# A fused attention and feed-forward kernel: strides, load rows, table loads and a new written order

## The chip, the cores and the metric

The kernel runs on one core of a Trainium2 chip, in one launch. The metric is the device time of an execution in microseconds (us); the number compared is the median over repeated executions. Before the change it is 213.36 us, the median of three (212.89, 213.36, 214.8). A separate execution was recorded by the hardware profiler, and all lines of profile in this text come from such records.

Names: TensorE (PE in the profile, PEld for its weight loads), VectorE (DVE), ScalarE (ACT), GpSimd (POOL), SyncE (SP). A name with a q (SPq, ACTq) is an engine's sequencer, which among other things issues DMAs.

## The reference

q, k and v are [8, 8, 576, 64] (batch, heads, positions, head size) in fp32. Each head's scores decay with distance; then a feed-forward layer runs over all 4608 tokens, with 512 columns in, 1024 inside and 512 out.

```python
scores = (1 / np.sqrt(64)) * np.matmul(q, k.transpose(0, 1, 3, 2))
gamma = 1.0 - 2.0 ** (-5.0 - np.arange(H))
Dmat = np.where(rel >= 0, gamma[:, None, None] ** rel[None, :, :], 0.0)   # rel = row - column
x = np.matmul(scores * Dmat, v)             # then [4608, 512], heads side by side
h = x @ w_in
e = np.exp(h - h.max(-1, keepdims=True))
solu = h * (e / (e.sum(-1, keepdims=True) + 1e-09))
ln = (solu - solu.mean(-1, keepdims=True)) / np.sqrt(var + 1e-06) * g_ln   # var: of solu over the row
out = ln @ w_out
```

## The kernel before

**Tiling.** The tokens are cut into 18 pairs n of 256 (two neighbouring positions on a partition): sixteen pairs of one batch entry each, and two tails (n = 8 and n = 17) that hold the last 64 positions of four entries. Each pair is worked through in two halves of 128 tokens (i = 0 or 1). The attention is done in chunks: products inside a chunk, plus a running state per head that is carried from chunk to chunk. The state gives the long-range part.

**Steps.** Each step is a short function, and a text called ORDER lists all of them, about a thousand words, in one sequence. A word is a step's name, its indices, and an engine letter where there is a choice: `q:0.1@v` is the cast of q of pair 0, half 1, on VectorE (v), ScalarE (s) or GpSimd (g). A loop at the end calls the steps in the order of the text. Each engine executes its own instructions strictly in that order; between engines semaphores are placed where data or buffers require it. So the order on each engine and on each DMA queue is written out by hand, and no scheduler changes it.

The steps that matter here:

- `lq`, `lk`, `lv` load 512 KB of q, k or v of a pair (L173, from SyncE's queue); `wi:a` loads 128 rows of w_in (L647), `wo:a` two blocks of rows of w_out (L667). The loads share 16 buffers.
- `q`, `k`, `v` cast to fp16 (L152 and L150 are the copy helper, L197 multiplies by a decay from the table `small`).
- `tp` transposes q and k of a pair on TensorE (L239), `qkT` copies the result to SBUF; `sc` are the scores (L265), `mk` the causal mask (L276, VectorE); `kp` the chunk's contribution to the state (L290); `t`, `s32`, `s16` the state itself, in fp32 and fp16; `xs` (L349) and `xv` (L364) the two products that make x; `xT` copies it to SBUF.
- `mm1` is x @ w_in (L426, L416), `max` its negated row maximum (L434), `exp` the exponential (L449), `solu` the product h * e (L497), `nmu` the negated mean (L507), `sq` the sum of squares (L517), `w1`, `w2`, `pow` the scale of a row.
- `lpj` transposes (L584), `uTj` copies, `mm2` is the second product (L607), `osb` scales its rows and `st` stores them (L634, L639). The last half is done in two halves of columns (`mm2:17.1.0`, `mm2:17.1.1` and so on).
- `cwA`, `cwB` cast one quarter of w_in in two halves (cast_w_in, through the copy helper); `ws` multiplies blocks of w_out by g_ln, `mean` and `mc` take their mean, `cw` subtracts it; `g32` scales g_ln.
- `warm:k` issues k products of zeros, 128x128 by 128x512, into a bank that nothing reads (L726). The zeros are the last slice of the tile s16s, which VectorE clears (L853).
- `gx` fills a table of decays with four exponentials on ScalarE (L734).

**Layout of w_in and w_out.** Before, the cast of w_in also permutes its 1024 columns: column 8p + c goes to place 128c + p, so the cast reads fp32 numbers 32 bytes apart. To match, row 8p + c of w_out is on partition p, in block c; a load of two blocks reads 4 KB in one piece per partition. g_ln is loaded as [128, 8] with 8 numbers in a row per partition.

**Start.** Ahead of the loop stand two loads from ScalarE's queue, `small` (L850) and g_ln (L851), then the constants: the clearing of s16s, `ones` and `mhalf` on VectorE, and `place`, `ident` (identity for the transposes) and `tris` (causal masks) on GpSimd. ORDER starts after that.

Of the kernel before, what the change touches and what calls it, by code (L numbers as in the profile page):

```python
# [12 lines left out]
P = 128  # L13
# [33 lines left out]
def kernel(  # L47
# [62 lines left out]
    T = {}  # L110
# [552 lines left out]
    @step  # L663
    def wo(a, i, j, eng):
        t = load_tile("wo").rearrange("p (c m) -> p c m", c=2)
        w = moe_w_out.rearrange("(p c) m -> p c m", p=P)
        nc.sync.dma_start(out=t, in_=w[:, 2 * a : 2 * a + 2])  # L667
        T["w_out32", 2 * a], T["w_out32", 2 * a + 1] = t[:, 0], t[:, 1]
# [50 lines left out]
    @step  # L719
    def warm(k, i, j, eng):  # L720


        junk = psum[:, int(BANKS[turns.get("bank", -1) + 1])]
        zeros = s16s[:, 2 + 6 - 1].rearrange("p a e d -> p (a e d)")
        for _ in range(k):
            nc.tensor.matmul(  # L726
                out=junk, lhsT=zeros[:, 0:P], rhs=zeros, start=True, stop=True
            )
# [3 lines left out]
    def gx_(n, i, j, eng):  # L732
# [12 lines left out]
        lk:0 gx lq:0 k:0.0@s k:0.1@g q:0.0@v lv:0 lq:1 q:0.1@v warm:21 tp:0 v:0.1@v v:0.0@v kp:0  # L745
        q:1.1@v t:0.0@v s32:0.0 qkT:0.1@v qkT:0.0@s lk:1 k:1.0@v q:1.0@g warm:6 sc:0.0 t:0.1 wi:2
        k:1.1@s sc:0.1 wi:0 wi:3 s32:0.1 mk:0.1.0 warm:4 tp:1 mk:0.0.0 mk:0.0.1 cwB:2@s s16:0.0@s
        mk:0.1.1 xv:0 cwA:2@g wi:1 qkT:1.1@v cwA:0@v cwB:0@g xT:0.0@v cwB:3@g qkT:1.0@s sc:1.0
        mk:1.0.1 xs:0.1 cwA:3@s mm1:0.0.3 lv:1 cwA:1@g xT:0.1@v s16:0.1@g cwB:1@s v:1.1@g mk:1.0.0
        sc:1.1 mm1:0.0.0 lq:2 lk:2 q:2.1@g q:2.0@g mk:1.1.0 mm1:0.1 v:1.0@v mk:1.1.1 k:2.0@g  # L750
        max:0.1 exp:0.1 mm1:0.0.2 mm1:0.0.1 max:0.0 k:2.1@v kp:1 t:1.0@s warm:7 tp:2 s32:1.0 lv:2
        solu:0.1 v:2.1@v exp:0.0 s16:1.0@g qkT:2.1@s qkT:2.0@s t:1.1 v:2.0@g nmu:0.1 solu:0.0
        xs:1.1 lq:4 xv:1 lv:3 lq:3 lk:3 xT:1.0@s nmu:0.0 warm:2 sc:2.1 sc:2.0 mk:2.1.0 xT:1.1@s
        kp:2 q:4.1@g q:4.0@g s32:1.1 mk:2.0.0 t:2.0@s mk:2.1.1 mk:2.0.1 uc:0.1@s sq:0.1 mm1:1.1
        s32:2.0 uc:0.0@v sq:0.0 max:1.1 xv:2 mm1:1.0 q:3.0@v xT:2.0@s exp:1.1 s16:2.0@g t:2.1
        xs:2.1 max:1.0 xT:2.1@s solu:1.1 mm1:2.0 lpj:0 q:3.1@g max:2.0 wo:2 wo:0 v:3.0@g g32
        k:3.1@g exp:1.0 mm1:2.1 solu:1.0 ws:4@s k:3.0@s wo:1 exp:2.0 w1:0@g v:3.1@g ws:0@g wo:3
        ws:1@g ws:5@g ws:2@s w2:0 uTj:0.1@v uTj:0.0@v ws:3@s max:2.1 lk:4 w1:1@v nmu:1.1 nmu:1.0
        ws:6@s warm:4 kp:3 ws:7@g t:3.0@s tp:3 solu:2.0 uc:1.0@v mm2:0.0 s32:3.0 qkT:3.0@s exp:2.1
        s32:2.1 qkT:3.1@s lv:4 pow:0 t:3.1 k:4.1@s sq:1.0 mean k:4.0@g sc:3.1 sc:3.0 solu:2.1  # L760
        nmu:2.0 mm2:0.1 v:4.1@v mc@s mk:3.1.0 mk:3.1.1 s16:3.0@g v:4.0@g lk:5 lk:6 mk:3.0.1
        mk:3.0.0 sq:1.1 uc:1.1@s tp:4 s32:3.1 kp:4 lq:5 qkT:4.0@s cw:5@g xv:3 qkT:4.1@s osb:0.1@v
        xs:3.1 t:4.0 warm:4 lpj:1 xT:3.1@s lq:6 cw:6@v sc:4.0 k:6.1@g nmu:2.1 xT:3.0@v s32:4.0
        k:5.1@g lv:5 uTj:1.1@s s16:1.1@s cw:0@v uTj:1.0@s osb:0.0@s t:4.1 mk:4.0.0 uc:2.0@v mm1:3.0
        w2:1 k:5.0@g q:5.1@g mm1:3.1 q:5.0@g pow:1 v:5.0@g s16:4.0@g max:3.0 uc:2.1@v s32:4.1 lk:7
        sc:4.1 q:6.0@s q:6.1@s mk:4.0.1 v:5.1@g mm2:1.0 exp:3.0 max:3.1 st:0.1 lv:6 mk:4.1.0
        mk:4.1.1 mm2:1.1 xv:4 w1:2@g xs:4.1 v:6.0@g solu:3.0 k:6.0@s v:6.1@g osb:1.0@s exp:3.1
        solu:3.1 dt:5 kp:5 t:5.0 osb:1.1@s xs:4.0 tp:6 st:1.0 s16:2.1@g cw:1@v st:0.0 sq:2.0 kp:6
        xT:4.1@s t:6.0 warm:2 lpj:2 s32:5.0 qkT:6.1@v t:5.1 xT:4.0@s qkT:6.0@s uTj:2.1@s cw:4@g
        sc:5.1 sc:5.0 uTj:2.0@s nmu:3.1 lq:8 mk:5.1.1 cw:7@v mk:5.1.0 sq:3.1 k:7.0@s sq:2.1 cw:3@v  # L770
        mk:5.0.0 mm1:4.0 max:4.0 lv:8 cw:2@g w2:2 pow:2 s32:6.0 mm1:4.1 s16:5.0@g exp:4.0 s16:6.0@g
        lq:7 mm2:2.1 lv:7 max:4.1 mk:5.0.1 solu:4.0 t:6.1 mm2:2.0 exp:4.1 k:7.1@s xs:5.1 xs:5.0
        osb:2.1@s solu:4.1 q:7.1@g sc:6.0 q:7.0@g osb:2.0@s mk:6.0.1 xv:5 v:7.1@v lk:8 lq:9 sc:6.1
        lpj:3 xT:5.0@s mm1:5.0 mk:6.1.0 uTj:3.0@s mk:6.0.0 mk:6.1.1 xs:6.0 lpj:4 nmu:3.0 w1:3@v
        max:5.0 uTj:3.1@s sq:3.0 xT:5.1@s xv:6 dt:7 xT:6.0 w2:3 xs:6.1 s32:5.1 q:8.0@g q:8.1@g
        mm2:3.1 v:8.0@g st:1.1 v:7.0@g nmu:4.1 mm2:3.0 w1:4@g k:8.1@g pow:3 q:9.0@g exp:5.0 xT:6.1
        uTj:4.1@v kp:7 uTj:4.0@s k:8.0@s lk:10 solu:5.0 osb:3.0@s nmu:5.0 sc:7.0 s16:5.1@g tp:8
        t:7.0 osb:3.1@s mm1:5.1 mk:7.0.0 sq:5.0 qkT:8.0@v nmu:4.0 sq:4.1 qkT:8.1@s sq:4.0 sc:7.1
        mk:7.0.1 lv:9 s32:7.0 mm1:6.0 max:5.1 exp:5.1 s16:7.0@g mk:7.1.1 mk:7.1.0 max:6.0 lk:9
        st:2.0 exp:6.0 st:2.1 s16:4.1@g q:9.1@g s16:3.1@g mm2:4.0 xs:7.0 s32:6.1 t:7.1 w2:4 pow:4  # L780
# [24 lines left out]
        solu:11.0 sq:9.1 s32:13.0 w2:9 nmu:10.1 pow:9 xv:12 t:13.1 sc:13.1 xT:12.0 xs:12.1 v:14.0@g
# [43 lines left out]
    with tc.manual_schedule():  # L849
# [63 lines left out]
```

## Time and profile before

| | |
|---|---|
| median of three executions | 213.36 us |
| profiled execution | 214.05 us, of which the span from first to last instruction is 212.3 us |
| TensorE busy | 196.4 us (93%), 3154 products |
| VectorE busy | 186.1 us (88%) |
| ScalarE busy | 171.0 us (81%) |
| GpSimd busy | 143.6 us (68%) |
| mean granted clock of TensorE | 0.983 |

Busy time of a group of instructions, from the table of groups with shapes kept apart (line, engine, operation, shapes, count, then busy us and mean ns of one, then idle time ahead of them and what ended it):

```profile
L434 DVE TENSOR_REDUCE nm<-psum 128x1 f32<-128x1024 f32 x35 | 42.5, 1218 | 6.5 <-PE psum L426 6.1
L726 PE MATMUL psum<-s16s 128*128 128x512 f16 x50 | 14.2, 429 | 3.5 <-DVE s16s L853 3.1 <-DVE u L497 0.4
L152 POOL CAST w_in<-ld 128x512 f16<-128x512 f32 x4 | 4.4, 1115 | 0.8 <-DMA ld<-in_moe_w_in_dram 0.8
L150 ACT CAST w_in<-ld 128x512 f16<-128x512 f32 x3 | 3.4, 1122 | 1.6 <-DMA ld<-in_moe_w_in_dram 1.6
```

A busy share is an average over the whole span. A matmul's end is modelled, and neighbours overlap, so the distance between the starts of two products says more than their length. Idle time of an engine that is not the bound in its stretch costs nothing.

### The profile page before, as it was taken

The page shows a single profiled execution, that of the slowest core. Times are in us where ns is not written, and L with a number is a line of the kernel's source. Part 1 is how long each engine was busy: PE and PEld are TensorE (multiplying, and loading weights), DVE is VectorE, ACT ScalarE, POOL GpSimd, SP SyncE. Part 2 cuts the span into 40 slices and gives each one's busy share as a digit, 9 for nine tenths or more (in the row PEclk, how much of TensorE's full clock was granted, in tenths as well). Part 3 has the DMA queues.
Part 4 walks back from the last instruction along what each step waited for, and adds up shares of the span by engine and source line. Part 5 has one row for each costly group of instructions (what it writes and reads, how often), then busy time and mean ns, then how long its engine had stood idle before and what let it go on. Part 6 is the DMA issues. An engine that isn't in the chain of part 4 may idle for free.

```text
span 212.3 us, 7613 instructions
## 1 busy us (share of the span) xinstructions
PE 196.4 (93%) x3154; PEld 103.2 (49%) x3154; DVE 186.1 (88%) x335; ACT 171.0 (81%) x288; POOL 143.6 (68%) x223
## 2 busy tenths in 40 slices
PE   4978979989998998999989999999999999999991
PEld 1444344445545464554645454645655555444450
DVE  3499699999998999898979999999998999798960
ACT  4265199989997988898987789999999769948971
POOL 7168689999999999879895494986665981001130
PEclk9996799999999999999999999999999999999999
DMA  6999999999488899999999989999999969564355
GB/s 162 290 383 310 281 296 367 295 259 262 138 217 183 213 209 216 320 293 223 249 327 164 285 236 316 279 197 246 264 203 217 238 99 179 171 148 115 85 198 150
DMA packets 90530, 49.29 MB, mean 232 GB/s; under 512 B 29440, under 2 KB 84992, under 8 KB 90496
## 3 DMA queue, kind: packets, MB, share of 16 engines
q1 hardware_dynamic: 90128, 48.70, 92.0%
q8 instruction: 24, 0.39, 0.8%
q10 hardware_dynamic: 368, 0.11, 0.4%
q14 instruction: 10, 0.08, 0.1%
HBM read 32.55 MB, written 9.44 MB: 198 GB/s over the span
## 4 chain that ended last, share of the span: by engine, by line
PE 70%; DVE 14%; DMA 4%; SPq 4%; issue 3%; ACT 2%; POOL 1%; ACTq 0%; DVEq 0%; POOLq 0%
PE psum L426 25%; PE psum L607 24%; PE psum L265 5%; DVE nm L434 4%; PE psum L364 4%; DMA ld<-in_moe_w_in_dram 4%; PE psum L349 3%; PE psum L584 3%; SPq L173 3%; DVE u L497 2%; PE psum L290 2%; PE psum L239 1%; SPq L647 1%; PE psum L726 1%; DVE uc L553 1%
## 5 line engine op out<-in xcount | busy, mean ns | idle before, releaser
L426 PE MATMUL psum<-w_in,xT 128*128 128x512 f16 x280 | 68.5, 390 | 1.6 <-issue 0.7
L607 PE MATMUL psum<-w_out,uTj 128*128 128x512 f16 (+1 forms) x248 | 55.1, 372 | 0.0
L434 DVE TENSOR_REDUCE nm<-psum 128x1 f32<-128x1024 f32 x35 | 42.5, 1218 | 6.5 <-PE psum L426 6.1
L449 ACT ACTIVATE e<-psum,nm 128x1024 f32<-128x1024 f32 x35 | 39.0, 1114 | 11.0 <-DVE nm L434 9.2
L607 PEld LDWEIGHTS <-uTj 128*128 128x128 f16 x296 | 28.0, 98 | 31.0 <-issue 0.6
L497 DVE SCALAR_TENSOR_TENSOR u<-psum,e 128x1024 f16<-128x1024 f32 x35 | 42.0, 1216 | 0.4 <-ACT e L449 0.3
L517 ACT ACTIVATE sq<-u,nmu 128x1024 f16<-128x1024 f16 x35 | 40.3, 1150 | 1.2 <-DVE nmu L507 0.9
L426 PEld LDWEIGHTS <-xT 128*128 128x128 f16 x280 | 25.8, 100 | 31.3 <-issue 4.7
L540 POOL TENSOR_TENSOR rs<-w,mhalf 128x2 f32<-128x2 f32 x17 | 11.8, 696 | 38.0 <-DVE w L528 36.7
L197 POOL TENSOR_TENSOR v<-ld,small 128x512 f16<-128x512 f32 x29 | 30.4, 1057 | 4.6 <-DMA ld<-in_v_dram 3.5
L197 POOL TENSOR_TENSOR qk<-ld,small 128x512 f16<-128x512 f32 x24 | 25.0, 1050 | 1.1 <-DMA ld<-in_q_dram 0.6
L150 ACT COPY uTj<-psum 128x1024 f16<-128x1024 f16 (+1 forms) x18 | 17.3, 990 | 3.1 <-PE psum L584 3.1
L314 POOL TENSOR_TENSOR s32a<-t,small 128x256 f32<-128x256 f32 x16 | 10.6, 662 | 11.8 <-DVE t L152 6.9
L726 PE MATMUL psum<-s16s 128*128 128x512 f16 x50 | 14.2, 429 | 3.5 <-DVE s16s L853 3.1
L152 POOL CAST qk<-ld 128x512 f16<-128x512 f32 x25 | 15.4, 628 | 0.7 <-DMA ld<-in_k_dram 0.6
L150 ACT COPY qkT<-psum 128x1024 f16<-128x1024 f16 x12 | 12.0, 1018 | 4.7 <-PE psum L239 4.7
L265 PE MATMUL psum<-qkT 64*64 64x128 f16 x576 | 14.7, 223 | 0.2
L150 ACT CAST xT<-psum 128x512 f16<-128x512 f32 x24 | 13.3, 588 | 1.7 <-PE psum L349 1.0
L265 PEld LDWEIGHTS <-qkT 64*64 64x64 f16 x576 | 9.8, 107 | 7.5 <-issue 6.3
L364 PEld LDWEIGHTS <-v 64*64 64x64 f16 x576 | 9.3, 106 | 7.1 <-issue 6.8
L349 PE MATMUL psum<-qkT,s16s 128*128 128x128 f16 (+1 forms) x128 | 10.7, 216 | 1.6 <-POOL s16s L152 1.4
L314 POOL TENSOR_TENSOR s32b<-t,small 128x256 f32<-128x256 f32 x16 | 10.2, 640 | 2.0 <-DVE t L305 1.8
(263 smaller groups left out, 337.2 us busy)
## 6 DMA issues: line engine op xcount, KB each, us to landing
ld<-in_k_dram SPq DMA_DIRECT2D x16, 512.0 KB, 7.7
ld<-in_q_dram SPq DMA_DIRECT2D x16, 512.0 KB, 7.2
ld<-in_v_dram SPq DMA_DIRECT2D x16, 512.0 KB, 7.1
ld<-in_moe_w_in_dram SPq DMA_DIRECT2D x4, 512.0 KB, 7.5
ld<-in_moe_w_out_dram SPq DMA_DIRECT2D x4, 512.0 KB, 7.0
ld<-in_q_dram SPq DMA_DIRECT2D x8, 128.0 KB, 4.4
ld<-in_v_dram SPq DMA_DIRECT2D x8, 128.0 KB, 4.8
ld<-in_k_dram SPq DMA_DIRECT2D x8, 128.0 KB, 3.9
```

The lines of the kernel that those rows point to most:

```text
L150: nc.scalar.copy(out=out, in_=in_)
L197: vec(eng).tensor_tensor(out=to, in0=src, in1=tab[:, 8 * e : 8 * e + 8].unsqueeze(2).to_broadcast([P, H, D]), op=ALU.mult,)
L265: nc.tensor.matmul(out=s[o][cc, hp], lhsT=qkT_view(n, 1, c)[dd, e, hp], rhs=qkT_view(n, 0, c)[dd, :, hp], start=True, stop=True,)
L314: nc.gpsimd.tensor_tensor(out=s, in0=T["t", n, i], in1=gs.unsqueeze(2).to_broadcast([P, 4, D]), op=ALU.mult)
L349: nc.tensor.matmul(out=to, lhsT=state[:, hp].rearrange("p e d -> p (e d)"), rhs=rhs, start=first and hp == 0 and j == 0, stop=True, skip_g ...
L364: nc.tensor.matmul(out=x[c][oo, hp], lhsT=v16[cc, e, 2 * hp + o], rhs=T["ret", n, e, o][cc, hp], start=first[c] and e == 0 and hp == 0, st ...
L426: nc.tensor.matmul(out=h[:, a], lhsT=s[:, d], rhs=w_in16[:, d, a * 512 : (a + 1) * 512], start=r == 1, stop=r == 4,)
L434: nc.vector.tensor_reduce(out=nm, in_=T[key("h", n, i, j)], axis=AX.X if j is not None else AX.XY, op=ALU.max, negate=True)
L449: nc.scalar.activation(out=flat(e, j), in_=T[key("h", n, i, j)], func=ACT.Exp, bias=T["nm", n, i], accum_out=s)
L497: nc.vector.scalar_tensor_tensor(out=flat(u, j), in0=T[key("h", n, i, j)], scalar=1.0, in1=flat(T[key("e", n, i, j)], j), op0=ALU.mult, op ...
L517: nc.scalar.activation(out=t, in_=T[key("u", n, i, j)], func=ACT.Square, bias=T["nmu", n, i], accum_out=ss)
L607: nc.tensor.matmul(out=o, lhsT=T["uT", n, i][:, c], rhs=wt[:, c, a : a + w], start=c == 0, stop=c == NF - 1,)
```

## The change

Four edits and a new ORDER. All products with values, and all instructions on data, are there before and after; which engine does a cast changes in places.

1. The casts of w_in read and write without a stride; columns keep their order. Block c of w_out is then rows 128c to 128c + 127, one row per partition, and g_ln is loaded with number 128c + p on partition p.

```diff
     def cast_w_in(a, i, eng):
-        src = T["w_in32", a].rearrange("p (f c) -> p c f", c=NF)[:, 4 * i : 4 * i + 4]
-        copy(eng, w_in16[:, a, 512 * i : 512 * i + 512].rearrange("p (c f) -> p c f", c=4), src)
+        copy(eng or "s", w_in16[:, a, 512 * i : 512 * i + 512], T["w_in32", a][:, 512 * i : 512 * i + 512])
...
     def wo(a, i, j, eng):
         t = load_tile("wo").rearrange("p (c m) -> p c m", c=2)
-        w = moe_w_out.rearrange("(p c) m -> p c m", p=P)
+        w = moe_w_out.rearrange("(c p) m -> p c m", p=P)
```

2. `small` and g_ln become steps in ORDER and are issued from SyncE's queue.

```diff
+    @step
+    def small_(n, i, j, eng):
+        nc.sync.dma_start(out=small, in_=nc.inline_tensor(small_np, name="small_c").ap())
+
+    @step
+    def gln_(n, i, j, eng):
+        with nc.allow_non_contiguous_dma("1024 numbers"):
+            nc.sync.dma_start(out=gln, in_=moe_g_ln.rearrange("(c p) -> p c", p=P))
...
     with tc.manual_schedule():
-        nc.scalar.dma_start(out=small, in_=nc.inline_tensor(small_np, name="small_c").ap())
-        nc.scalar.dma_start(out=gln, in_=moe_g_ln.rearrange("(p c) -> p c", p=P))
```

3. The constants become two steps in ORDER: `consts` (place, the clearing of s16s, ones, mhalf, ident) and `tris`. Their instructions are the same.

4. ORDER is written anew, with a new list of PSUM banks. Its beginning:

```diff
-        lk:0 gx lq:0 k:0.0@s k:0.1@g q:0.0@v lv:0 lq:1 q:0.1@v warm:21 tp:0 v:0.1@v v:0.0@v kp:0
-        q:1.1@v t:0.0@v s32:0.0 qkT:0.1@v qkT:0.0@s lk:1 k:1.0@v q:1.0@g warm:6 sc:0.0 t:0.1 wi:2
-        k:1.1@s sc:0.1 wi:0 wi:3 s32:0.1 mk:0.1.0 warm:4 tp:1 mk:0.0.0 mk:0.0.1 cwB:2@s s16:0.0@s
-        mk:0.1.1 xv:0 cwA:2@g wi:1 qkT:1.1@v cwA:0@v cwB:0@g xT:0.0@v cwB:3@g qkT:1.0@s sc:1.0
+        tris lv:0 lq:0 small lk:0 q:0.1@v k:0.1@v q:0.0@v k:0.0@s v:0.1@g consts v:0.0@g lq:1
+        q:1.0@g warm:19 tp:0 q:1.1@v kp:0 t:0.0@v qkT:0.1@v qkT:0.0@s warm:6 sc:0.0 lk:1 wi:2
+        s32:0.0 sc:0.1 k:1.0@v s16:0.0@g k:1.1@g t:0.1 mk:0.1.1 wi:0 mk:0.1.0 cwA:2@s cwB:2@s
+        warm:7 tp:1 mk:0.0.1 wi:3 mk:0.0.0 xs:0.1 warm:3 xv:0 qkT:1.1@s qkT:1.0@v wi:1 cwB:0@v
+        cwA:0@v s32:0.1 xT:0.1@s sc:1.0 xT:0.0@s cwA:3@g mk:1.0.0 warm:2 sc:1.1 mm1:0.0.2 cwB:3@g
+        mk:1.1.1 mk:1.0.1 mk:1.1.0 cwA:1@s cwB:1@g mm1:0.1 lv:1 mm1:0.0.1 mm1:0.0.0 lq:2 lk:2
+        v:1.1@v v:1.0@g q:2.1@g s16:0.1@g kp:1 max:0.1 mm1:0.0.3 gx q:2.0@v k:2.0@g lv:2 exp:0.1
...
```

Products of zeros, in order: before 21, 6, 4, 7, 2, 4, 4, 2 (50); after 19, 6, 7, 3, 2, 10, 4 and seven times 2 (65). On TensorE the first 19 stand ahead of tp:0, as the 21 did. On VectorE the first instructions become q:0.1, k:0.1, q:0.0, then the clearing of s16s. `gln` stands on SyncE's queue between lq:3 and lv:3. `gx` stands on ScalarE between cwA:1 and exp:0.1. The end of ORDER becomes `osb:17.1.0@s osb:17.1.1@v st:17.1.1 st:17.1.0`, where both halves were scaled on ScalarE.

## The prediction

> **What bounds the kernel now.** I read the page's span in slices first, then the timeline of the first 30 us, then busy time by stretch, then the chain of waits.
>
> ```profile
> PE   4978979989998998999989999999999999999991
> ...
> DVE  3499699999998999898979999999998999798960
> ...
> PEclk9996799999999999999999999999999999999999
> ```
>
> A slice is 5.3 us. TensorE is short of full only in the first third; its granted clock has one dip, slices 4 and 5. The timeline (start, us, engine, line, operation, idle before and releaser) shows the start:
>
> ```profile
> 1.29 1.76 DVE L853 MEMSET s16s<- 128x2048 uint32 x1 [1.29 <-PEq L897]
> ...
> 3.11 6.77 PE L726 MATMUL psum<-s16s 128*128 128x512 f16 x21 [3.11 <-DVE s16s L853]
> ...
> 5.36 0.61 POOL L152 CAST qk<-ld 128x512 f16<-128x512 f32 x1 [0.57 <-DMA ld<-in_k_dram]
> ...
> 7.22 1.29 DVE L197 TENSOR_TENSOR qk<-ld,small 128x512 f16<-128x512 f32 x2 [4.02 <-DMA ld<-in_q_dram]
> 7.34 2.04 PEld L726 LDWEIGHTS <-s16s 128*128 128x128 f16 x10 [0.27 <-issue]
> 8.95 1.29 DVE L197 TENSOR_TENSOR v<-ld,small 128x512 f16<-128x512 f32 x2 [0.44 <-DMA ld<-in_v_dram]
> 9.81 0.52 PEld L239 LDWEIGHTS <-qk 64*128 64x128 f16 x32 [0.42 <-issue]
> ```
>
> VectorE clears s16s before any load lands, so the 21 zero products of L726 fill TensorE's wait and the first transposes (tp:0) start at 9.81. Loads land one by one: 5.36, 7.22, 8.95, some 1.8 us apart. Before 7.34 zero products start 0.427 us apart, after it 0.216.
>
> ```profile
> 20.00:25.00 5.00, 5.00 (x21) 1.80 (x14) 3.17 (x5) 0.00 (x0) 4.28 (x6) 0.56 1.14 286
> ...
> 35.00:40.00 5.00, 4.91 (x56) 2.54 (x55) 5.00 (x8) 4.98 (x11) 5.00 (x7) 1.00 1.06 332
> 40.00:50.00 10.00, 9.02 (x138) 4.38 (x138) 10.00 (x19) 9.31 (x16) 9.55 (x13) 1.00 1.04 271
> 50.00:60.00 10.00, 9.39 (x193) 5.07 (x188) 10.00 (x17) 9.67 (x17) 9.64 (x12) 1.00 0.69 178
> ...
> 90.00:100.00 10.00, 10.00 (x142) 5.23 (x141) 9.10 (x18) 9.17 (x16) 8.61 (x17) 1.00 0.95 271
> ```
>
> Columns: length, PE, PEld, DVE, ACT, POOL busy, granted clock, DMA share, GB/s. VectorE is full from 35 to 60; TensorE is full from 90 on. The chain says the same in order: to 51 us mostly VectorE steps, from about 82 us nearly all TensorE, one matmul behind the other. So the end is set by when the start lets VectorE go, then VectorE's work to about 80 us, then TensorE's remaining work, which no edit changes (every product with values is still there).
>
> **The change, step by step.** Times are against the profiled execution, 214.05 us (span 212.3 and 1.75 around it), which is 0.69 above the median, 213.36.
>
> *Where the zeros start.* In the new order VectorE casts q:0.1, k:0.1, q:0.0 and only then clears s16s; every zero product reads s16s, and 19 of them stand ahead of tp:0 on TensorE. SyncE now issues v, q, the tables, k. By the rows v lands at 5.36 and q at 7.22. The tables' 128 packets are an eighth of a load's 1024, 1.8/8 = 0.2 us, so they land about 7.4, and k behind them at 8.95 + 0.2 = 9.15. VectorE waits for k: cast 0.4, q:0.0 0.65, clear 1.76, so s16s is zero at 12.0. 19 products cost 4.23 us slow (3.11 to 7.34, ten of them) and 9 x 0.216: 6.2 us. tp:0 starts at 18.2, against 9.81: 8.4 us later. Queued behind the clear are q:1.1 and, through the zeros, all of TensorE; ScalarE and GpSimd wait in turn for tp:0 and kp:0. The Trainium skill, "TensorE: Matmul & The Clock Gate", Part 1, says that the slow time is a matter of a free-running window of about 3.4 us, not of a number of products; by it an estimate for the 19 is 5.8 to 7.5 us (one to two windows slow), which would move the sum by -0.4 to +1.3; the trace's 4.23 lies between.
>
> *What is caught up by 30 us.* In before, tp:0 to the first solu took from 9.81 to 27.19, with waits for late casts of w_in (0.5 of TensorE, 17.43 to 18.61 in the chain) and ten products of mm1:0 at 0.427 instead of 0.216 (2.1 us; granted clock 0.50 from 18 to 24). In the new order w_in has landed by 19 us (18.8 in before, +0.2) and is cast before its products, and zeros (6, 7, 3, 2) fill the gaps between 19 and 26, so I count the clock full. VectorE's own sum from t:0.0 (after kp:0, 19.25) to solu:0.1: t 0.34, qkT 0.6, k:1.0 0.42, t 0.34, four mk 2.4, qkT 0.6, two casts of w_in 0.84, four mk 2.4, v:1.1 0.69, max 1.14, q:2.0 0.69, max 1.14 = 11.6; waits for sc:0.1 0.5 and for sc:1 and mm1 0.3; and beside a busy GpSimd some of its instructions are long (k:1.0 1.26 for 0.42 at 12.51, v:1.0 1.53 for 0.69 at 20.85), nothing to 0.84, I take 0.4. Sum 12.8, so solu:0.1 starts about 32.0 at most and 31.2 at least, against 27.19: I take 4.5 us late. Of 8.4 us, 3.9 are caught up.
>
> *From there to 82 us.* VectorE is full in both. To solu:2.1 the new list holds xT:1.1 0.6, ws:4 0.7 and w1:0 0.15 more, q:3.0 0.8 and w1:1 0.15 less: +0.5; before idles 0.5 there, which a late start fills. After it one more w_out cast (0.86) stands on VectorE, and 0.9 us of idle at 67 can be filled. Sum 0: the 4.5 stay, with -1 to +1.
>
> *Casts of w_in without stride.* ScalarE 1.12 to 0.61 (three), GpSimd 1.11 to 0.63 (four, now three), VectorE 0.61 once to 0.42 twice. All end before 27 us while products wait for tp:0, so nothing is gained on the path; uncovered they were worth the 0.5 above, counted there.
>
> *Rows of w_out, g_ln and tables.* Each w_out load is 256 runs of 2 KB instead of 128 of 4 KB; issue to landing was 7.0 us, from 27.7, and the first use came at 38.8: 0 under those 4 us, up to 0.3 each if they were gone. g_ln becomes 1024 packets of 4 bytes instead of 128 of 32, on SyncE's queue behind lq:3, ahead of lv:3. In the first 40 us a small packet on ScalarE's queue took 29 ns and one on SyncE's 40 (share times 16 engines over packets), so 1.9 to 2.6 us for loads behind it. They land some 30 to 33 us; g32 is GpSimd's turn at about 35, behind s32:1.1; 0, and 2.4 if that cover fails, with q:3.1 and s16:2.0 queued behind g32. The Trainium skill, "DMA: Bandwidth & Descriptors", Specifications, says a transfer below 512 B is a read-modify-write, which speaks against this edit; an estimate by it, two passes for one, doubles the 2.4 to 4.8 and would add about 2 us of stall; no row here has 4-byte runs. gx (1.65) moves from 4.33 to ahead of exp:0.1, where ScalarE waited 5.96 for max; 0, or 0.5 if max is sooner. tris goes ahead and ident behind v:0.1, ready by 9.3, under the zeros.
>
> *More zeros.* 65 instead of 50, 15 x 0.216 = 3.2 us, all between 22 and 55 us where TensorE waits for VectorE; 0, at most 1 where VectorE's wait is for TensorE.
>
> *Tail.* The last two halves are scaled on ScalarE and VectorE side by side; in before the second (208.12) waited behind ScalarE's DMA issue, with its product done at about 207.8: -0.3. A loss needs VectorE to be late there, which idles.
>
> Sum: 4.5 + 0 - 0.3, less 0.2 for idle that may fill: +4.0. 214.05 + 4.0 = 218.05, on the median 217.4.
>
> **Rivals.** (a) *TensorE absorbs the lag.* From 30 to 80 us it idles 3.4 us (the stretches' remainders) and runs 12 zeros (2.6 us); were it and not VectorE that sets the pace, the 4.5 would vanish there: 213.1. Against: VectorE's 10.00 of 10 us. (b) *Not slower: the new order keeps VectorE clear of GpSimd.* The long instructions between 12 and 75 us (k:1.0 and v:1.0 0.84 each, two w2 0.9 and 0.85, q:3.0 0.19, v:4.1 0.35, two w_out 0.25 and 0.35, two uc 0.25 and 0.39) hold 5.2 us. If none stays, 217.4 - 5.2 = 212.2; it decides once less than 1.2 us stay. Against: GpSimd is as full (9.5 of 10) and the mix is the same. A sum of (a) and (b) alone would be over 1% faster. (c) *Slower still: the clock falls again*, as at 17.8 us in before, when the gaps around xv:0 and mm1:0 outweigh the zeros: +2.1, 219.5; a g32 stall of 2.4 on top 221.9. For it: mk holds xv:0 whatever the zeros. The Trainium skill, same page and part, has a rule for it (an idle window halves the clock); by this trace it did so once, after TensorE's 0.61 and 0.26 busy of 1 us at 14 and 15. (d) *The clear does not hold the zeros*, if it ran ahead of the casts all the same: tp:0 then waits for q:0.0 only, 10.3, 0.5 late, and the 2.6 (0.5 and 2.1) is caught up: 217.4 - 4.5 + 0.5 - 2.6 = 210.8. Against it: VectorE runs its list in order all through the timeline.
>
> **Chances.** Forecast 0.62 (215.5 to 219.4); (c) 0.20; (a) or a half of (b) 0.10; (b) nearly whole or with (a) 0.05; (d) 0.03. One per cent, 2.1 us, is about what a measurement of this kernel tells from no change. Slower 0.82, same 0.12, faster 0.06. The range leaves out (b), (d) and the far end of (c): 214.2 to 221.0.
>
> **What would show it.** Zero products from about 12 us, released by the clear; tp:0 near 18; solu:0.1 near 31.7; VectorE full from 31 to 85; clock full from 17 us on; GpSimd waiting for g_ln at most briefly. Zeros starting before 9 us, or VectorE idle over 2 us between 32 and 80, would make it wrong.

## The result, and the profile after

The changed kernel takes **222.19 us** (median of four executions, 221.28 to 223.19); the kernel before, run beside it, 213.12 us (212.08 to 214.80). The ratio is 1.0456, with a 95% interval of 1.0403 to 1.051. The forecast of 217.4 us had the direction, and named the right start of it, but was 4.8 us too low; the top of its range, 221.0, is passed too. The profiled execution of the changed kernel took 222.34 us, its span 220.4: 8.3 and 8.1 us more than before's 214.05 and 212.3. Ratios compare undisturbed executions alone, so they can differ a little from the quotient of two medians.

The span of the changed kernel in 40 slices, of 5.5 us here:

```profile
PE   0089989999987989999987999999999999999991
...
DVE  0423999999999899999996999999998999799960
...
PEclk9999999999999999999999999999999999999998
```

TensorE does nothing in the first two slices, where it had zero products to run before. After that both engines are as full as they were, and the dip of the granted clock is gone: most of the loss was made at the start, and not by the clock.

The timeline of the changed kernel's first 34 us (start, us, engine, line, operation, in brackets the idle time before and its releaser):

```profile
7.03 0.69 DVE L197 TENSOR_TENSOR qk<-ld,small 128x512 f16<-128x512 f32 x1 [7.03 <-DMA small<-small_c]
...
8.67 0.43 DVE L152 CAST qk<-ld 128x512 f16<-128x512 f32 x1 [0.95 <-DMA ld<-in_k_dram]
...
10.08 1.76 DVE L729 MEMSET s16s<- 128x2048 uint32 x1 [0.38 <-issue]
...
11.90 7.11 PE L764 MATMUL psum<-s16s 128*128 128x512 f16 x19 [11.90 <-DVE s16s L729]
...
18.93 0.64 PE L239 MATMUL psum<-ident,qk 64*128 64x64 f16 x32
...
20.00 0.42 DVE L152 COPY t<-psum 128x256 f32<-128x256 f32 x1 [7.41 <-PE psum L290]
...
24.98 2.50 DVE L152 CAST w_in<-ld 128x512 f16<-128x512 f32 x2
...
33.26 1.21 DVE L497 SCALAR_TENSOR_TENSOR u<-psum,e 128x1024 f16<-128x1024 f32 x1
```

VectorE waits for two loads, then clears s16s. The 19 zeros wait for the clear; tp:0 waits for the zeros; VectorE then stands idle for 7.41 us, because t:0.0 waits for kp:0 behind tp:0. Further down stand two casts of w_in that together take 2.50 us. solu:0.1, the last line, starts at 33.26; before it started at 27.19.

Where the difference grows can be read from the starts of the 35 products `solu` (L497) in both traces:

| step | before, us | after, us | later by |
|---|---|---|---|
| tp:0 (first transpose) | 9.81 | 18.93 | 9.1 |
| solu:0.1 | 27.2 | 33.3 | 6.1 |
| solu:2.0 | 44.6 | 51.2 | 6.6 |
| solu:7.0 | 103.0 | 109.1 | 6.1 |
| solu:8.0 | 114.2 | 121.7 | 7.5 |
| solu:12.0 | 152.1 | 160.3 | 8.2 |
| solu:17.0 | 197.8 | 206.0 | 8.2 |
| end of the span | 212.3 | 220.4 | 8.1 |

From 33 to 109 us nothing is lost or caught up on balance (on the way the lag lies between 5.2 and 7.2 us). Busy time by stretch of the changed kernel (columns as in the prediction: length, PE, PEld, DVE, ACT, POOL, granted clock, DMA share, GB/s) says why:

```profile
35.00:40.00 5.00, 4.94 (x115) 2.78 (x113) 5.00 (x11) 4.60 (x8) 4.81 (x8) 1.00 1.09 342
40.00:50.00 10.00, 9.90 (x166) 4.95 (x164) 10.00 (x17) 8.89 (x16) 9.64 (x13) 1.00 1.05 268
...
90.00:100.00 10.00, 9.97 (x109) 4.69 (x107) 9.44 (x19) 8.82 (x16) 6.77 (x13) 1.00 1.12 311
```

VectorE is full first, TensorE later, as in before; neither has slack in which a late start could be made up.

Between solu:7.0 and solu:8.0 1.4 us more are lost. The timeline of TensorE there, in the changed kernel (the products of kp:9):

```profile
114.67 0.38 PE L290 MATMUL psum<-v,qk 64*64 64x64 f16 x22
...
116.91 0.28 PE L290 MATMUL psum<-v,qk 64*64 64x64 f16 x10 [1.86 <-issue]
```

and in the kernel before:

```profile
108.65 1.25 PE L426 MATMUL psum<-w_in,xT 128*128 128x512 f16 x5
110.64 0.82 PE L426 MATMUL psum<-w_in,xT 128*128 128x512 f16 x3 [0.74 <-issue]
```

In the middle of 32 equal products that need nothing new, TensorE stops for 1.86 us and waits for nothing that the profile shows ("issue"). Before, there was such a stop behind the fifth product of mm1:7.1, the step after kp:9, of 0.74 us. The prediction had no term for it. The second group of experiments asks what it is.

### The profile page after: what moved, and what is told of

It is laid out like the page before. It is cut to its first block, busy times and chain, and to the rows that moved or that the text cites. A ratio compares the mean times of both kernels' runs of the same rounds, so it can differ in the third digit from the quotient of the medians.

```text
span 220.4 us, 7632 instructions
## 1 busy us (share of the span) xinstructions
PE 197.1 (89%) x3169; PEld 103.5 (47%) x3169; DVE 189.3 (86%) x339; ACT 165.3 (75%) x280; POOL 143.9 (65%) x226
## 4 chain that ended last, share of the span: by engine, by line
PE 54%; DVE 36%; issue 4%; DMA 2%; SPq 1%; ACT 0%; DVEq 0%; ACTq 0%
PE psum L607 20%; PE psum L426 17%; DVE nm L434 7%; DVE u L497 6%; PE psum L764 4%; PE psum L265 3%; PE psum L364 3%; DMA ld<-in_k_dram 2%; DVE w_out L721 2%; PE psum L349 2%; PE psum L584 2%; PE psum L290 2%; DVE v L197 2%; DVE uc L553 1%; DVE w L528 1%
## 5 line engine op out<-in xcount | busy, mean ns | idle before, releaser
L426 PE MATMUL psum<-w_in,xT 128*128 128x512 f16 x280 | 65.9, 380 | 0.8 <-DVE ret__392 L276 0.7
L497 DVE SCALAR_TENSOR_TENSOR u<-psum,e 128x1024 f16<-128x1024 f32 x35 | 42.2, 1215 | 0.1
L197 POOL TENSOR_TENSOR v<-ld,small 128x512 f16<-128x512 f32 x30 | 31.6, 1057 | 4.4 <-DMA small<-small_c 3.1
L540 POOL TENSOR_TENSOR rs<-w,mhalf 128x2 f32<-128x2 f32 x17 | 12.7, 749 | 28.0 <-DVE w L528 16.5
L764 PE MATMUL psum<-s16s 128*128 128x512 f16 x65 | 19.2, 432 | 11.9 <-DVE s16s L729 11.9
L197 POOL TENSOR_TENSOR qk<-ld,small 128x512 f16<-128x512 f32 x24 | 25.6, 1072 | 1.6 <-PE psum L290 0.6
L314 POOL TENSOR_TENSOR s32a<-t,small 128x256 f32<-128x256 f32 x16 | 9.8, 612 | 21.4 <-DVE t L152 8.6
L150 ACT COPY qkT<-psum 128x1024 f16<-128x1024 f16 x13 | 13.0, 1020 | 13.0 <-PE psum L239 13.0
L152 POOL CAST qk<-ld 128x512 f16<-128x512 f32 x28 | 17.8, 642 | 0.3
L764 PEld LDWEIGHTS <-s16s 128*128 128x128 f16 x65 | 6.3, 109 | 19.6 <-DVE s16s L729 11.9
L150 ACT CAST qk<-ld 128x512 f16<-128x512 f32 x14 | 8.5, 629 | 6.6 <-DMA ld<-in_k_dram 6.6
L152 POOL CAST s16s<-s32a 64x256 f16<-64x256 f32 x26 | 11.4, 437 | 0.9
```

Source lines behind the costliest of these rows:

```text
L150: nc.scalar.copy(out=out, in_=in_)
L152: vec(eng).tensor_copy(out=out, in_=in_)
L197: vec(eng).tensor_tensor(out=to, in0=src, in1=tab[:, 8 * e : 8 * e + 8].unsqueeze(2).to_broadcast([P, H, D]), op=ALU.mult,)
L426: nc.tensor.matmul(out=h[:, a], lhsT=s[:, d], rhs=w_in16[:, d, a * 512 : (a + 1) * 512], start=r == 1, stop=r == 4,)
L497: nc.vector.scalar_tensor_tensor(out=flat(u, j), in0=T[key("h", n, i, j)], scalar=1.0, in1=flat(T[key("e", n, i, j)], j), op0=ALU.mult, op ...
L540: nc.gpsimd.tensor_tensor(out=rs, in0=w, in1=mhalf, op=ALU.pow)
```

## Experiments: the late clear

Twelve kernels were run, in three groups, each group with the kernel before on the same chip: 213.84 us (e1 to e4), 213.83 (e5 to e8) and 213.52 (e9 to e12), medians of 19, 19 and 25 executions. All times in one table; tp:0, solu:0.1 and span are from each profiled execution.

| kernel | median, us | ratio to before, 95% interval | tp:0 | solu:0.1 | span |
|---|---|---|---|---|---|
| after | 222.19 | 1.0456 (1.0403 to 1.051) | 18.93 | 33.3 | 220.4 |
| e1 clear first | 214.71 | 1.0027 (0.9982 to 1.0071) | 10.04 | 24.5 | 211.2 |
| e2 layout alone, on before | 213.27 | 0.9999 (0.9957 to 1.0042) | 9.46 | 25.2 | 211.7 |
| e3 clear late, on before | 220.59 | 1.0338 (1.0282 to 1.0393) | 17.81 | 33.4 | 218.7 |
| e4 casts of w_in off VectorE | 220.11 | 1.0280 (1.0212 to 1.0349) | 17.72 | 30.9 | 218.0 |
| e5 no first zeros | 211.18 | 0.9907 (0.9873 to 0.994) | 10.08 | 25.8 | 210.9 |
| e6 e1 and e4 together | 215.11 | 1.0040 (1.0003 to 1.0078) | 10.10 | 24.2 | 215.6 |
| e7 more zeros, on before | 215.75 | 1.0116 (1.0068 to 1.0165) | 9.46 | 24.9 | 213.5 |
| e8 e1 without first zeros | 211.20 | 0.9900 (0.9866 to 0.9933) | 10.06 | 25.2 | 209.2 |
| e9 fewer late zeros | 218.39 | 1.0252 (1.0181 to 1.0323) | 18.45 | 32.8 | 216.8 |
| e10 e8, code shifted | 213.99 | 1.0043 (1.0005 to 1.0081) | 10.02 | 25.6 | 212.0 |
| e11 no zeros at all | 211.79 | 0.9953 (0.9911 to 0.9996) | 10.05 | 25.1 | 209.8 |
| e12 before, no first zeros | 212.63 | 0.9992 (0.9948 to 1.0036) | 7.72 | 25.4 | 212.4 |

**e1: the changed kernel with the clear moved ahead of the loop**, where before had it.

```diff
     with tc.manual_schedule():
+        nc.vector.memset(s16s, 0.0)
...
-        nc.vector.memset(s16s, 0.0)
```

> The changed kernel with one instruction moved: the clear of s16s is VectorE's first instruction again. Theory A (the late clear sets the loss): zeros start at about 3.1 us, the first transposes at about 10 instead of 18.9, the first solu at 27 to 28 instead of 33.3; the 6 us of the start go, the 2 us lost between 105 and 121 us stay: 214 to 216. Theory B (the loss is in the rest of the new order, and TensorE would have waited anyway): 220 or more.

One moved instruction takes the loss away: ratio 1.0027, and 214.71 us lies in the expected 214 to 216. The timeline of e1:

```profile
3.11 6.99 PE L763 MATMUL psum<-s16s 128*128 128x512 f16 x19 [3.11 <-DVE s16s L889]
...
10.04 0.64 PE L239 MATMUL psum<-ident,qk 64*128 64x64 f16 x32
...
16.41 0.75 DVE L152 CAST w_in<-ld 128x512 f16<-128x512 f32 x2
...
17.60 1.17 POOL L152 CAST w_in<-ld 128x512 f16<-128x512 f32 x2 [2.49 <-DMA ld<-in_moe_w_in_dram]
...
24.46 1.21 DVE L497 SCALAR_TENSOR_TENSOR u<-psum,e 128x1024 f16<-128x1024 f32 x1
```

The same zeros now run while TensorE has nothing else. solu:0.1 is 8.8 us sooner than in the changed kernel and 2.7 sooner than before, where 27 to 28 was expected: up to there the new order itself is the better one. The two casts of w_in on VectorE, 2.50 us in the changed kernel, take 0.75 here, while GpSimd idles (for 2.49 us up to 17.60). In the changed kernel GpSimd multiplies fp32 tiles through the same time:

```profile
24.97 1.03 POOL L197 TENSOR_TENSOR v<-ld,small 128x512 f16<-128x512 f32 x1
...
25.97 1.22 POOL L197 TENSOR_TENSOR qk<-ld,small 128x512 f16<-128x512 f32 x1
```

By the end the lead has shrunk from 2.7 to 1.2 us of span.

**e3: the kernel before with its clear late**, behind q:0.1 and nothing else changed. It is the reverse of e1.

```diff
-        lk:0 gx lq:0 k:0.0@s k:0.1@g q:0.0@v lv:0 lq:1 q:0.1@v warm:21 tp:0 v:0.1@v v:0.0@v kp:0
+        lk:0 gx lq:0 k:0.0@s k:0.1@g q:0.0@v lv:0 lq:1 q:0.1@v clr warm:21 tp:0 v:0.1@v v:0.0@v kp:0
```

> The kernel before with one instruction moved: VectorE clears s16s after q:0.1, directly ahead of the 21 zeros. Theory A: s16s is zero at about 10.3 us, 21 zeros take 6.8 to 8, the first transposes start at 17 to 18 instead of 9.8, the first solu 4 to 6 us later than 27.2: 217 to 219. Theory B: 213 to 214.5.

```profile
8.92 1.76 DVE L733 MEMSET s16s<- 128x2048 uint32 x1 [0.38 <-issue]
...
10.74 7.14 PE L726 MATMUL psum<-s16s 128*128 128x512 f16 x21 [10.74 <-DVE s16s L733]
```

In the old order, too, the clear alone makes the kernel 3.4% slower. Its lag behind before is 6.2 us at solu:0.1 and stays between 6.0 and 6.7 through every later solu; the span is 6.3 longer. So nothing between 30 us and the end gives back a late start, and the loss of the changed kernel after 109 us is another matter. The size was underestimated here as well: TensorE does not make good what the expectation allowed it.

**e2: the unstrided casts, the rows of w_out and the pattern of g_ln, alone on the kernel before.**

```diff
-        src = T["w_in32", a].rearrange("p (f c) -> p c f", c=NF)[:, 4 * i : 4 * i + 4]
-        copy(eng, w_in16[:, a, 512 * i : 512 * i + 512].rearrange("p (c f) -> p c f", c=4), src)
+        copy(eng, w_in16[:, a, 512 * i : 512 * i + 512], T["w_in32", a][:, 512 * i : 512 * i + 512])
...
-        w = moe_w_out.rearrange("(p c) m -> p c m", p=P)
+        w = moe_w_out.rearrange("(c p) m -> p c m", p=P)
...
-        nc.scalar.dma_start(out=gln, in_=moe_g_ln.rearrange("(p c) -> p c", p=P))
+        with nc.allow_non_contiguous_dma("1024 numbers"):
+            nc.scalar.dma_start(out=gln, in_=moe_g_ln.rearrange("(c p) -> p c", p=P))
```

> The kernel before with the layout alone: casts of w_in without stride, rows 128c+p of w_out, g_ln with the matching pattern on ScalarE's queue, the old order. Theory A: these edits are hidden, 212 to 213.5 (0.5 us of TensorE's wait for the casts may go). Theory C (loads of 2 KB runs and 1024 packets of 4 bytes delay what is behind them): 215 or more, with w_out's or later loads landing late.

Ratio 0.9999: worth nothing. In its profiled execution the clock happened to stay full through mm1:0, so that solu:0.1 came 2.0 us sooner; 0.7 of that was left at the end. With the 1024 short packets of g_ln ahead of the loop, here on ScalarE's queue, three casts that wait for loads began some 0.75 us later than in before (7.98 instead of 7.22, 9.71 instead of 8.95, 11.50 instead of 10.76), a third of the 1.9 to 2.6 that the prediction allowed.

**e4: the changed kernel with two casts of w_in on ScalarE instead of VectorE.**

```diff
-        s32:0.0 sc:0.1 k:1.0@v s16:0.0@g k:1.1@g t:0.1 mk:0.1.1 wi:0 mk:0.1.0 cwA:2@s cwB:2@s
-        warm:7 tp:1 mk:0.0.1 wi:3 mk:0.0.0 xs:0.1 warm:3 xv:0 qkT:1.1@s qkT:1.0@v wi:1 cwB:0@v
-        cwA:0@v s32:0.1 xT:0.1@s sc:1.0 xT:0.0@s cwA:3@g mk:1.0.0 warm:2 sc:1.1 mm1:0.0.2 cwB:3@g
+        s32:0.0 sc:0.1 k:1.0@v s16:0.0@g k:1.1@g t:0.1 mk:0.1.1 wi:0 mk:0.1.0 cwA:2@s cwB:2@s cwA:0@s cwB:0@s
+        warm:7 tp:1 mk:0.0.1 wi:3 mk:0.0.0 xs:0.1 warm:3 xv:0 qkT:1.1@s qkT:1.0@v wi:1
+        s32:0.1 xT:0.1@s sc:1.0 xT:0.0@s cwA:3@g mk:1.0.0 warm:2 sc:1.1 mm1:0.0.2 cwB:3@g
```

> The changed kernel with the two casts of w_in's first block on ScalarE (after the two of block 2, in its idle time) instead of on VectorE, where they took 2.50 us beside a busy GpSimd. If these 2.4 us are part of the lag of 6.1: the first solu 1.5 to 2.4 us earlier, 220 to 220.7. If TensorE's late start holds mk and max all the same: 222, unchanged.

solu:0.1 is 2.3 us sooner than in the changed kernel, and the median 2.1 lower. Half of it is not the casts: the 19 zeros took

```profile
12.18 5.61 PE L764 MATMUL psum<-s16s 128*128 128x512 f16 x19 [12.18 <-DVE s16s L729]
```

5.61 us instead of 7.11, since six and not 13 of them ran slow to the end, and tp:0 began 1.2 sooner. The remaining 1.1 are put down to the casts; no run separates the two. **e6** puts both edits together, the early clear and the moved casts.

> The changed kernel with both repairs: the clear first, and the two casts of w_in's first block on ScalarE. If the casts cost VectorE only because the late start put them beside a busy GpSimd (0.75 for both with the clear first, 2.50 without), they cost nothing here: 214 to 215, as with the clear first alone. If VectorE's time counts there in any case: 0.7 less, 213.5.

It does not beat e1 (1.0040 against 1.0027, the intervals overlap): where the casts take 0.75 us instead of 2.50 there is nothing to gain from moving them. The profiled execution of e6 took 217.33 us, 2.2 above the median, so its place in the table stands for that execution only.

**e5: the changed kernel without its 19 first zeros; the clear stays late.**

```diff
-        q:1.0@g warm:19 tp:0 q:1.1@v kp:0 t:0.0@v qkT:0.1@v qkT:0.0@s warm:6 sc:0.0 lk:1 wi:2
+        q:1.0@g tp:0 q:1.1@v kp:0 t:0.0@v qkT:0.1@v qkT:0.0@s warm:6 sc:0.0 lk:1 wi:2
```

> The changed kernel without the 19 zero products ahead of the first transposes; the clear stays where the change has it. Theory A in its narrow form (the zeros are what carries the late clear to TensorE): the first transposes start at about 10 us, when q and k are cast; VectorE goes on after the clear at 12.6 instead of 20.0; what is lost is a clock at half in the first stages (2 to 4 us): 215.5 to 218. Rival (the half clock costs as much as the zeros did, or VectorE's clear alone holds the start): 220 or more.

11.0 us less than the changed kernel, and faster than before, much more than expected. The late clear alone costs nothing; it costs through the zeros that stand ahead of tp:0 and wait for it. The price of doing without them is a slow first transpose:

```profile
10.08 1.04 PE L239 MATMUL psum<-ident,qk 64*128 64x64 f16 x32 [10.08 <-POOL ident L733]
...
12.08 2.74 PE L764 MATMUL psum<-s16s 128*128 128x512 f16 x6 [0.34 <-DVE s16s L729]
```

1.04 us instead of 0.64; the next six zeros are slow too, and the granted clock is full from 15.1 us on. That tp:0 begins no sooner than with the zeros first (10.04 in e1) is due to `ident`, for which it waits; the prediction had it ready by 9.3. **e8** is e5 with the clear first (or e1 without the 19 zeros).

> The changed kernel with the clear first and without the 19 first zeros: TensorE is idle until the first transposes at 10 us. Theory: the zeros are of use only by the clock: the first stages run at half clock for 4 to 7 us of TensorE's time, 2 to 3 us late, 216 to 218; if the clock does not matter there: 214.7, as with the clear first alone.

211.20 us, as e5, and less than the expectation had either way: once no product ahead of tp:0 waits for the clear, its place is indifferent. These two are the fastest of all, 0.9 and 1.0% faster than the kernel before, with intervals of 0.6 to 1.3%. Against e1 this is not won at the start: tp:0 begins at 10.06 and 10.04, and solu:0.1 is even 0.7 us later in e8. Of the 2.0 us by which its span is shorter, 1.3 come between solu:7.0 and 7.1, where e1 stops in kp:9 for 1.13 us and e8 does not; the next experiments are about that stop.

## Experiments: TensorE's stops

**e7: seven more zeros in the kernel before**, to hold its clock up at 18 us.

```diff
-        mk:0.1.1 xv:0 cwA:2@g wi:1 qkT:1.1@v cwA:0@v cwB:0@g xT:0.0@v cwB:3@g qkT:1.0@s sc:1.0
-        mk:1.0.1 xs:0.1 cwA:3@s mm1:0.0.3 lv:1 cwA:1@g xT:0.1@v s16:0.1@g cwB:1@s v:1.1@g mk:1.0.0
+        mk:0.1.1 warm:5 xv:0 cwA:2@g wi:1 qkT:1.1@v cwA:0@v cwB:0@g xT:0.0@v cwB:3@g qkT:1.0@s sc:1.0
+        mk:1.0.1 xs:0.1 cwA:3@s warm:2 mm1:0.0.3 lv:1 cwA:1@g xT:0.1@v s16:0.1@g cwB:1@s v:1.1@g mk:1.0.0
```

> The kernel before with seven more zero products where its TensorE waits between 14.5 and 18.6 us: five ahead of xv:0, two ahead of the first of mm1:0. If the dip of the clock to 0.50 between 18 and 24 us costs time (2.1 us of products there): 0 to 2 us faster by how often the clock now stays full, 212 to 213. If VectorE and the loads of w_in set this stage: 213.8, unchanged; if the zeros hold up xv:0: 0.5 slower.

The clock stayed full, solu:0.1 came 2.3 us sooner than in before, and the lead was still 1.9 at solu:7.0. At solu:7.1 it was a lag of 1.1, which remained to the end: ratio 1.0116, slower than any of its expectations. In between TensorE stopped, in kp:9 again, but after its 30th product and not its 22nd:

```profile
106.38 0.42 PE L290 MATMUL psum<-v,qk 64*64 64x64 f16 x30
...
108.87 0.22 PE L290 MATMUL psum<-v,qk 64*64 64x64 f16 x2 [2.08 <-issue]
...
109.02 3.57 PE L426 MATMUL psum<-w_in,xT 128*128 128x512 f16 x8
```

The stop is 1.3 us longer than that of before. The eight products behind it take 3.57 us, where eight took 1.90 elsewhere: the granted clock is 0.50 from 109 to 112 us, and that costs the other 1.7 of the 3.0. In e6 a stop of 2.12 us in kp:9 was followed by 3.4 us at half clock too, and one of 0.77 us at 65.1 as well, with a wait of 0.65 for VectorE shortly before it; in the other kernels no stop of 1.86 us or less was.

So the place of the stop is not tied to one product. A count of TensorE's records (products, weight loads and two of its sequencer at the start) in each of the 14 traces gives the rule: the 28 stops of 0.3 us or more without a releaser begin after exactly 449, 1473, 1985, 2497 or 3521 records, which are multiples of 512 less 63. Not every kernel stops at each of these places (e8 at none), and the places at 961, at 3009 and beyond 3521 never show a stop. How many zeros a kernel has ahead of such a place decides which product it falls on. The length varies at one and the same product: 1.1 to 2.1 us over the five kernels that stop behind the 22nd product of kp:9, 0.5 to 1.3 over the three that stop behind the fifth of mm1:7.1. The list of DMA queues has one kind beside the loads and stores that fits; over the whole changed kernel, and for 114.2 to 115.6 us alone (queue, kind: packets, MB, share of 16 engines):

```profile
q8 instruction: 24, 0.39, 0.8%
```

```profile
q8 instruction: 1, 0.02, 5.4%
```

24 transfers for the page's 6338 instructions on TensorE (3169 products and as many weight loads), one for each 256 or so. Why only multiples of 512 show a stop, the traces leave open. The one at kp:9 begins at 114.34 and takes 5.4% of 16 x 1.4 us, 1.2 us; it has landed at 115.54, and TensorE goes on at 116.91. In all 28 stops TensorE resumes 1.2 to 1.7 us after such a transfer has landed. In e8 and e9, which have no stop at 3521, the transfer had landed 1.8 and 1.5 us before TensorE came to that place. The theory: TensorE had run out of instructions. By it the place is bad in kp:9, as its 64 short instructions are used up in 0.4 us. Four runs test it.

**e9: the changed kernel without its last 18 zeros** (the four ahead of xs:1.1, and seven times two).

```diff
-        t:1.0@s s32:1.0 max:0.0 k:2.1@s warm:10 tp:2 s16:1.0@g solu:0.1 exp:0.0 warm:4 xs:1.1 lq:3
-        t:1.1 xv:1 v:2.0@g qkT:2.0@s qkT:2.1@s solu:0.0 xT:1.0@s v:2.1@v xT:1.1@v warm:2 kp:2
+        t:1.0@s s32:1.0 max:0.0 k:2.1@s warm:10 tp:2 s16:1.0@g solu:0.1 exp:0.0 xs:1.1 lq:3
+        t:1.1 xv:1 v:2.0@g qkT:2.0@s qkT:2.1@s solu:0.0 xT:1.0@s v:2.1@v xT:1.1@v kp:2
...
```

> The changed kernel without its last 18 zero products (from the four ahead of xs:1.1 on); the clear stays late and the 19 ahead of tp:0 stay. In every run so far TensorE's stalls without a releaser begin after the same number of its instructions in the trace (1985, 2497, 3521, each a multiple of 512 less 63), just behind a transfer on the profile's instruction queue. Theory (TensorE runs out of instructions, because a load of 256 of them lands too late): 36 instructions fewer move the place of the 1.86 us stall from behind the 22nd product of kp:9 to behind ten more products of kp:9 and eight of mm1:7.1, 1.8 us of products, so that it all but vanishes; the lag behind before is about 6 us from the first solu to 105 us and does not grow there; about 220.3 us. Rival 1 (the stall belongs to kp:9 or to what other engines do there): it stays behind the 22nd product of kp:9, 222.2. Rival 2 (the late zeros hold the clock up): the granted clock falls between 33 and 90 us, over 222.5.

The stop is gone:

```profile
113.27 0.44 PE L290 MATMUL psum<-v,qk 64*64 64x64 f16 x32
...
113.65 1.90 PE L426 MATMUL psum<-w_in,xT 128*128 128x512 f16 x8
```

The lag behind before does not grow between solu:7.0 and 7.1 but falls, from 4.7 to 3.7 us, where the changed kernel's grew from 6.1 to 7.2: 2.1 us of difference at this place. The median is 218.39, lower than the 220.3 expected: 0.5 us come from a shorter start of the 19 zeros (6.56 us), and 0.9 more are gained by solu:7.0. These 0.9 are not the work of the zeros: at solu:3.1, behind all the late zeros, the gain is still 0.4; it comes after 70 us, where the changed kernel stops for 0.56 us at 1985 records and e9 does not. The clock stayed full, which rules out the second rival.

**e10: e8, which had no stop, with 19 short products of zeros added**, so that the code behind them has the positions of e1.

```diff
+    def shift(k, i, j, eng):
+        junk = psum[:, int(BANKS[turns.get("bank", -1) + 1])]
+        zeros = s16s[:, 2 + 6 - 1].rearrange("p a e d -> p (a e d)")
+        for _ in range(k):
+            nc.tensor.matmul(out=junk[:, 0:64], lhsT=zeros[:, 0:P], rhs=zeros[:, 0:64], start=True, stop=True)
...
-        t:1.0@s s32:1.0 max:0.0 k:2.1@s warm:10 tp:2 s16:1.0@g solu:0.1 exp:0.0 warm:4 xs:1.1 lq:3
+        t:1.0@s s32:1.0 max:0.0 k:2.1@s shift:19 warm:10 tp:2 s16:1.0@g solu:0.1 exp:0.0 warm:4 xs:1.1 lq:3
```

> The version with the clear first and without the 19 zeros (211.2 us, no stall at kp:9), plus 19 short products of zeros with 64 columns ahead of tp:2, where TensorE waits for VectorE; they bring the later instructions back to the positions that they have with the 19 zeros. Theory (late instruction loads): the stall is back behind the 22nd product of kp:9, 1.0 to 2.0 us long, and the time is 212.2 to 213.3. Rival (the stall belongs to the work): no stall over 0.3 us there, and 211.2 (at most 211.7).

TensorE in e8, and then in e10:

```profile
105.48 0.45 PE L290 MATMUL psum<-v,qk 64*64 64x64 f16 x32
105.86 1.90 PE L426 MATMUL psum<-w_in,xT 128*128 128x512 f16 x8
```

```profile
106.80 0.38 PE L290 MATMUL psum<-v,qk 64*64 64x64 f16 x22
108.74 0.28 PE L290 MATMUL psum<-v,qk 64*64 64x64 f16 x10 [1.57 <-issue]
```

The stop is back, behind the 22nd product. The 19 products took 0.72 us at 24 us; the median rose by 2.8, to 213.99, more than expected. Of the 2.8 us by which its span is longer than e8's, 1.3 are there at solu:7.0, and 1.8 come between solu:7.0 and 7.1. That the position of an instruction decides where TensorE stops is thereby shown by adding and by removing. That the late transfer is the cause rests on its time and count; no run here speeds it up.

**e11: e8 without any zeros**, all the remaining 46 left out of ORDER.

> The new order with the clear first and no zero products anywhere. Theory (the zeros earn nothing in this order): clock full by 20 us but for one stretch of 3 to 4 us, solu:0.1 at 25 to 26, 210.5 to 212. Rival (they hold the clock in the gaps between 20 and 35 us): the clock falls to half once more there, solu:0.1 at 27 to 28, 213 to 215.

The clock did fall once more, to 0.50 from 27.7 to 31.1 us (0.77 on average in the stretch from 25 to 30 us and 0.89 in the next), as the rival had it; but solu:0.1 came at 25.1 and the median is 211.79, as the theory had it. Its interval overlaps that of e8. In this order 65 products of zeros earn nothing that can be measured.

**e12: the kernel before without its 21 first zeros.**

```diff
-        lk:0 gx lq:0 k:0.0@s k:0.1@g q:0.0@v lv:0 lq:1 q:0.1@v warm:21 tp:0 v:0.1@v v:0.0@v kp:0
+        lk:0 gx lq:0 k:0.0@s k:0.1@g q:0.0@v lv:0 lq:1 q:0.1@v tp:0 v:0.1@v v:0.0@v kp:0
```

> The kernel before without its 21 zeros ahead of tp:0 (the clear is first there anyway). Theory (first zeros not needed in either order): tp:0 starts between 9.2 and 9.9, is slow for some 3 us longer, and the 42 instructions fewer move the stall of 0.74 us behind the fifth product of mm1:7.1 to work at which it is hidden: 212 to 213.3. Rival (the zeros hold the clock for the transposes and the products up to 18 us): 214.5 to 216.5.

212.63 us is within what the theory expected, but tp:0 began at 7.72, not between 9.2 and 9.9: even in before the zeros held its first products up by 2.1 us. The profiled execution took 214.15 us, 1.5 above the median. In it the lead of 1.7 at solu:0.1 falls to 0.4 by solu:1.1, with the clock at 0.50 from 28.7 to 32.1 us, is 1.8 again at solu:8.1, with no stop at 3521, and is lost between solu:8.1 and 13.0; why is open. The ratio of 0.9992 says that the first zeros neither help nor hurt in the old order.

## Why the prediction was right, and where it was wrong

- **Where the zeros start: right.** 12.0 us predicted, 11.90 measured, released by the clear. A little luck is in it: k was there 0.5 us sooner, and VectorE then stood idle for 0.38 ahead of the clear. Their length was not: 6.2 predicted, 7.11 measured. The prediction took the slow stretch from before (4.23 us, ten products); here 13 products were slow, until 17.76, which is 5.86 us. The same stretch lasted 4.7 in e9 and 2.9 in e4, with the same 19 products. This speaks for the rule that the prediction cites from the Trainium skill ("TensorE: Matmul & The Clock Gate", Part 1), that the slow time follows a window of its own and not a number of products; its estimate of 5.8 to 7.5 us held 7.11 and e9's 6.56, and just missed e4's 5.61, whose slow stretch of 2.9 is shorter than the window of 3.4 in that rule. Where the clock falls again later (e3, e6, e7, e11, e12), it stays at half for 3.4 us each time, and for twice that in before. So the 19 products should have stood in the sum as a range, not as one value. tp:0 thus came 9.1 late instead of 8.4.
- **"What is caught up by 30 us": the step that failed first.** Of 8.4 us 3.9 were to be caught up; of 9.1 it was 3.0. The step allowed VectorE 0.84 us for two casts of w_in and 0.4 for long instructions beside a busy GpSimd; these two casts alone took 2.50. e4 gives about 1.1 us to them. It had this price in its own text: instructions of VectorE that GpSimd stretched by 0.84 each. Other terms were too high, the waits above all (0.8 allowed, 0.25 measured), so that the stretch from t:0.0 to solu:0.1 took 13.3 us against 12.8; and the forecast took less than its own 12.8, which would have made it 4.9 late. Sum at solu:0.1: 6.1 late, not 4.5.
- **"From there to 82 us": right.** 0, with -1 to +1, was predicted: 6.1 at 33 us, 6.1 at 109, with swings of about 1 us between. e3 shows the same with nothing else changed. Rival (a) falls with it.
- **"TensorE's remaining work, which no edit changes": the step that failed second.** The products are the same, but their place in TensorE's code is not: with 15 zeros more the stop at 3521 records falls into kp:9 and grows from 0.74 to 1.86 us, 1.1 of the 1.4 us that had been added by solu:8.0. The clue was in the list of TensorE's waits in before (line that waited, releaser: us in total, times, longest), and it was passed over:

```profile
PE psum L584 <- issue: 0.9, 1, 0.9
...
PE psum L426 <- issue: 0.7, 1, 0.7
PE psum L364 <- issue: 0.7, 1, 0.7
```

- **More zeros: right for their work, wrong for their place.** 0, at most 1, was predicted. The late zeros as work cost nothing that e9 shows; by shifting the stops they cost 0.9 us by solu:7.0 and 2.1 at kp:9.
- **Casts without stride, rows of w_out, g_ln, tables: right.** 0 predicted, e2's ratio is 0.9999. g_ln was issued at 20.84 (1.74 us of SyncE), landed 7.3 us later, at 28.2, and g32 ran at 36.36 without a wait: the cover held. gx was hidden, as predicted.
- **Tail:** -0.3 predicted; from solu:17.0 to the end it is -0.2.
- **Rivals.** (b) fell: the longest instruction beside a busy GpSimd, the pair of casts of w_in, is one that the new order made. (c) gave a time near the right one (219.5 to 221.9) for a wrong reason: the clock was full from 18 us on, and g32 never waited. (d) fell at the third line of the timeline: the clear ran behind the casts.

The sum, in the profiled executions: 4.0 predicted; 1.6 more at solu:0.1; 0.2 of idle time that did not fill; 1.4 at kp:9 and around it; 0.7 more by solu:12.0, whose cause is open (in e9 it is 0.5); 0.1 less gained in the tail; 0.2 outside the span (1.94 instead of 1.75). Together 8.2, where 8.3 was measured.

## What to carry to other kernels

Products that only keep TensorE busy must neither stand ahead of real work nor read something that another engine has yet to write; here most of the loss went through 19 of them, and the changed kernel without them beats both, though part of its lead over before is a stop of TensorE that it does not have: 1.0 of e8's 3.1 us of span comes between solu:7.0 and 7.1, and e10, with the stop back, is no faster than before. When an instruction is moved behind a wait on its engine, list every reader of what it writes, and count what the reader's own queue then holds back. And before a difference of 1% is put down to an edit, look for TensorE's stops without a releaser: adding or removing a few instructions moves them.

## What was not expected of the hardware

- **Running out of instructions.** TensorE stops for up to 2.1 us at places that go by the count of its instructions. As far as times and counts tell, it has used up its code before the next 16 KB (0.39 MB in 24 transfers) are there. The Trainium skill ("Runtime: NRT & Kernel Launch", Instruction fetch mechanics) says that instructions come in blocks of 256 by a queue of their own, and that the cost of crossing a block is mostly hidden. The count of 24 transfers agrees, and so does "mostly": before shows three such stops, the changed kernel two, e8 none. What is not hidden is dear all the same: 2.4 us of stops in before (0.90, 0.73 and 0.74), 2.4 in the changed kernel, and 4.0 in e7 (1.30, 0.66 and 2.08 at 1985, 2497 and 3521).
- **Two equal casts on VectorE took 0.75 us in e1 and 2.50 us in the changed kernel.** The shapes are the same; in the changed kernel GpSimd is busy through all of it, in e1 it idles.
- **A clock at half speed cost little.** Without the first zeros tp:0 took 1.04 us instead of 0.64, and six later zeros 2.74 instead of 1.47. The zeros that were to avoid this took 7. In e1 and e8 tp:0 begins at the same time, with the zeros and without; solu:0.1 is 0.7 us later without.
